# A recurrent attention stage on one Trainium2 core: which PSUM banks the gate exponents, the carried state's output and the output transposes share

## The chip, the core and the metric

One core of a Trainium2 chip runs the whole program. Five engines work in order, each through its own queue: TensorE (PE in the profile, with its weight loads as PEld), VectorE (DVE), ScalarE (ACT), GpSimd (POOL) and SyncE (SP, which only issues DMAs here; ACT's queue and POOL's issue some too). The metric is the device time of one execution in microseconds.

## The reference, cut to what matters

The first of three parts is a gated linear recurrence with a stabiliser; the other two (a routed expert layer and a two-branch product layer) run behind it and are not touched.

```python
m_new = np.maximum(f_gate[:, :, t] + m, i_gate[:, :, t])
f_stab = np.exp(f_gate[:, :, t] + m - m_new)
i_stab = np.exp(i_gate[:, :, t] - m_new)
C = f_stab[:, :, None, None] * C + i_stab[:, :, None, None] * np.einsum('bhd,bhe->bhde', vt, kt)
n = f_stab[:, :, None] * n + i_stab[:, :, None] * kt
h_tilde = np.einsum('bhde,bhe->bhd', C, qt)
denom = np.maximum(np.abs(nq), 1.0)          # nq = n . q
y[:, :, t] = o * h_tilde / denom             # o = sigmoid(o_gate)
```

There are 4 batches, 8 heads, 768 positions and 40 columns per head. The result, seen as 3072 tokens of 320 columns, goes into the router and the experts.

## The kernel before

The positions are cut into 6 chunks of 128. A step n (0 to 23) works on batch b = n mod 4 of chunk c = n // 4. Within a chunk the recurrence is a masked 128x128 product per head; the state carried from the chunk before adds its own part. One Python loop writes the order by hand: in step n the first two stages of step n+1 run beside the last stages of step n, the output of step n-2 is transposed and the router's logits of step n-3 are computed. No scheduler reorders anything, so every engine executes exactly what the loop wrote, and an instruction that waits stops all that is behind it on its engine.

The names that the text uses, with their lines:

- pe (L397) is the gate difference of four heads, one 512-column matmul; dd (L399, ACT) is its exponential, which POOL masks (L400). pq (L405) is q times k of the same heads, and P (L408, DVE) the product of pq and dd. Each step has two halves of all that (heads 0 to 3 and 4 to 7); they are called pe0, dd0, P0 and pe1, dd1, P1 here.
- pg (L421) is what the carried state gives, eight matmul records for four products; DVE scales it into num (L423).
- pv (L436) is P times v, pst (L442) the new state; DVE adds and copies them (L445, L453), and ACT spreads the state for the next chunk (Cb, L460).
- px (L485) are the output transposes of step n-2, copied by ACT to xt (L487, L488); pl (L495) are the logits of step n-3, copied by DVE into L (L496), the last DVE instruction that belongs to a step.
- pgt (L368, L369) are the gate transposes of the next chunk. They run in a gate step, the last of each chunk (n = 3, 7, 11, 15, 19); ACT copies them to gt (L371).
- Beside the steps the later layer's weights are converted from 64-bit words (`convs`, L119 to L153): DVE works on mu (L119, L122, L125), ACT rounds it (L131 or L152), POOL subtracts (L134, L136 or L153), and then DVE may start the next one. The gates of the next chunk (L293 to L358) run in the same gaps; ACT's hi (L316) and est (L353) belong to them.

PSUM has eight banks and all are taken: pst 1, pe 1, pq 2, pg 1, pv 1, and two for the tag `pxt`, which px, pl and pgt share. A tile that is allocated from a tag gets one of its buffers and has to wait until the last reader of the tile that was there has finished.

Of the kernel before, what the change touches and what calls it, by code (L numbers as in the profile page):

```python
# [6 lines left out]
F32 = mybir.dt.float32  # L7
# [14 lines left out]
T = 128  # L22
NC = S // T
DE = D + 1
# [19 lines left out]
class Kern:  # L44
# [173 lines left out]
    def attention(self, es):  # L218
# [6 lines left out]
        ps = es.enter_context(tc.tile_pool(name="aps", bufs=1, space=PSUM))  # L225
# [3 lines left out]
        def load_g(c):  # L229
            t = ld.tile([128, 2, T], F32, name="fi", bufs=2)  # L230
            nc.sync.dma_start(t, a["fi4"][:, c])
            FI[c] = t
# [28 lines left out]
        def load(n):  # L261
            c, b = divmod(n, B)
            t = qr[n % NQ]
            bd = t[:, H:].rearrange("p (a s) t -> p a s t", s=2)
            for s in range(2):
                r, rs = slice(64 * s, 64 * s + D), slice(D * s, D * s + D)
                nc.sync.dma_start(t[r, 0:H], a["qk"][rs, c, b])
                nc.sync.dma_start(bd[r, :, s], a["qk"][rs, c, b, 0:4])
            v_ = ld.tile([128, H, DE + D], F32, name="vk")
            nc.sync.dma_start(v_, a["vk"][b, c])  # L270
            VK[n] = v_

        def load_o(c):
            o_ = ld.tile([128, B, DM], F32, name="og", bufs=2)
            SG[c] = o_
            self.dma(lambda: nc.scalar.dma_start(o_, a["og"][:, c]))

        def sig(c):
            nc.scalar.activation(SG[c], SG[c], AF.Sigmoid)
            nc.scalar.activation(warm, gs[0:1, 0:1], AF.Exp)  # L280
# [83 lines left out]
        def gates2(c):  # L364
            est, mov, EW, md = GA[c]
            pg = ps.tile([128, 2 * T + 16], F32, tag="pxt", name="pgt", bufs=2)
            for i in range(2):
                nc.tensor.transpose(pg[:, i * T:(i + 1) * T], EW[:, i], identf)  # L368
            nc.tensor.matmul(pg[:, 2 * T:], psel, md, start=True, stop=True)  # L369
            gt = wk.tile([128, 2 * T + 16], F32, name="gt")  # L370
            nc.scalar.activation(gt, pg, AF.Copy)  # L371
            GA[c] = (est, mov, gt)

        def pre(n):
            c, b = divmod(n, B)
            est, mov, gt = GA[c]
            if c < NC - 1:
                wa = gt[:, T + 32 * b:T + 32 * b + 8]
                dec = gt[:, 2 * T + 4 * b:2 * T + 4 * b + 4]
                wv = wk.tile([128, H, DE], F32, name="wv")  # L380
                nc.gpsimd.tensor_tensor(wv, VK[n][:, :, 0:DE], wa[:, :, None].to_broadcast([128, H, DE]),
                                        op=OP.mult)
                ct = None
                if c:
                    ct = wk.tile([128, 4, DE], F32, name="ct")
                    nc.gpsimd.tensor_tensor(ct, Cc[:, b], dec[:, :, None].to_broadcast([128, 4, DE]), op=OP.mult)
                ST[n] = (wv, ct)

        def s1(n):
            c, b = divmod(n, B)  # L390
            est, mov = GA[c][0:2]
            qk = qr[n % NQ]
            P = wk.tile([128, H, T], F32, name="P", bufs=2)
            PT[n] = P
            for g in range(2):
                pe = ps.tile([128, 4, T], F32, name="pe", bufs=1)
                nc.tensor.matmul(pe, est[:, b], mov[:, 4 * g:4 * g + 4, :], start=True, stop=True)  # L397
                dd = wk.tile([128, 4, T], F32, name="dd", bufs=2)
                nc.scalar.activation(dd, pe, AF.Exp)  # L399
                nc.gpsimd.affine_select(dd, dd, pattern=[[0, 4], [1, T]], compare_op=OP.is_ge, fill=0.0,  # L400
                                        base=0, channel_multiplier=-1)
                pq = ps.tile([128, 4, T], F32, name="pq", bufs=2)
                for hp in (2 * g, 2 * g + 1):
                    o = 2 * (hp - 2 * g)
                    nc.tensor.matmul(pq[:, o:o + 2], qk[:, 4 + hp], qk[:, H + 2 * hp:H + 2 * hp + 2],  # L405
                                     start=True, stop=True)
                yield
                nc.vector.tensor_mul(P[:, 4 * g:4 * g + 4], pq, dd)  # L408
                yield
# [3 lines left out]
        def s2g(n):  # L413
            c, b = divmod(n, B)
            num = wk.tile([128, H, DE], F32, name="num", bufs=3)
            ND[n] = num
            if c:
                ea = GA[c][2][:, 32 * b:32 * b + 8]
                pg = ps.tile([128, 4, 2, DE], F32, name="pg")
                for hp in range(4):  # L420
                    nc.tensor.matmul(pg[:, hp], qr[n % NQ][:, hp], Cb[:, b, hp], start=True, stop=True)  # L421
                yield
                nc.vector.tensor_tensor(num, pg.rearrange("p a b d -> p (a b) d"),  # L423
                                        ea[:, :, None].to_broadcast([128, H, DE]), op=OP.mult)
# [55 lines left out]
        def s3(n):  # L480
            xf = XF.pop(n)
            px = ps.tile([128, 3 * T], F32, tag="pxt", name="px", bufs=2)
            for j in range(3):
                w = min(128, DM - 128 * j)
                nc.tensor.transpose(px[0:w, j * T:(j + 1) * T], xf[:, 128 * j:128 * j + w], identf)  # L485
            xt = xtb[n % 2]
            nc.scalar.activation(xt[:, 0:2], px[:, 0:2 * T], AF.Copy)  # L487
            nc.scalar.activation(xt[0:64, 2], px[0:64, 2 * T:3 * T], AF.Copy)  # L488
            XT[n] = xt

        def s4(n):
            xt = XT.pop(n)
            pl = ps.tile([128, 96], F32, tag="pxt", name="pl", bufs=2)
            for j in range(3):
                nc.tensor.matmul(pl, xt[:, j], wg[:, j], start=(j == 0), stop=(j == 2))  # L495
            return lambda: nc.vector.tensor_scalar(self.L[:, n], pl[:, 0:E], 0.0, None, op0=OP.add)  # L496
# [5 lines left out]
        def fill(k):  # L502
            j = 0
            while k and j < len(bg):
                v = next(bg[j], None)
                if v is None:
                    bg.pop(j)
                elif v == "w":
                    j += 1
                else:  # L510
                    k, j = k - 1, 0
# [5 lines left out]
        NS = B * NC  # L517
# [17 lines left out]
        for n in range(NS):  # L535
            c, b = divmod(n, B)
            if n == 2:
                bg.append(m2)
            if True:
                if n + 2 < NS:  # L540
                    load(n + 2)
                if n == 1:
                    next(m2)
                if b == 3 and c + 1 < NC:
                    gates2(c + 1)
                    if c + 2 < NC:
                        bg.insert(0, gates(c + 2))
                        if c + 3 < NC:
                            load_g(c + 3)
                m = s1(n + 1) if n + 1 < NS else iter(())  # L550
                next(m, None)
                g = s2g(n)
                next(g, None)
                fill(2)
                next(m, None)
                next(m, None)
                if n == 0:
                    sig(0)
                if b == 3 and c + 1 < NC:
                    sig(c + 1)  # L560
                self.drain()
                self.flush(b < 3)
                next(g, None)
                next(m, None)
                if n + 1 < NS:
                    pre(n + 1)
                g = s2(n)
                next(g)
                if 0 <= n - 2:
                    s3(n - 2)  # L570
                next(g)
                lc = s4(n - 3) if n >= 3 else lambda: None
                fill(2)
                next(g)
                fill(1)
                next(g)
                fill(1)
                next(g, None)
                lc()
            if n:  # L580
                xout(n - 1)
                if n % B == 0 and n // B + 1 < NC:
                    load_o(n // B + 1)
            if n - 3 == 7 or n - 3 == 15:
                bg.insert(0, self.keys(*KT[(n - 3) // 8]))
            fill(1)
# [643 lines left out]
```

## Time and profile before

| what | us |
|---|---|
| median of 3 timed runs (lowest, highest) | 911.85 (911.6, 914.33) |
| the profiled execution itself | 908.33 |
| its span in the profile | 906.6 |
| PE, DVE, ACT, POOL busy in the span | 822.6, 538.4, 353.3, 415.9 |
| mean granted clock of TensorE | 0.955 of full speed |

The attention stage takes about the first 196 us; the experts follow and keep PE busy nearly throughout. The profiled execution is one run, and its span leaves out 1.73 us around it. A row of the timeline gives the start, the duration and, in brackets, how long the engine had been idle before it and which instruction ended that. In the windows each engine has its busy time and, in brackets, its instructions.

### The profile page before, as it was taken

How to read it: one execution, taken by the hardware profiler on the slowest of the kernel's cores; microseconds unless marked ns; L12 is line 12 of the kernel's file. 1: busy time of each engine (PE TensorE's matmuls, PEld its weight loads, DVE VectorE, ACT ScalarE, POOL GpSimd, SP SyncE). 2: the span in 40 equal slices, each digit the busy share in tenths (PEclk: the TensorE clock that was granted, in tenths of full speed). 3: DMA queues.
4: the chain of work that ended last, by engine and by line, in shares of the span. 5: the costliest groups of instructions: out<-in, count | busy, mean ns of one | idle time of the engine just before them, and what ended most of it. 6: DMA issues, size and time to landing. Idle time of an engine off the chain costs nothing.

```text
span 906.6 us, 15898 instructions
## 1 busy us (share of the span) xinstructions
PE 822.6 (91%) x5939; PEld 780.7 (86%) x5939; DVE 538.4 (59%) x1188; ACT 353.3 (39%) x720; POOL 415.9 (46%) x441
## 2 busy tenths in 40 slices
PE   4889889976888799989989999999999999999996
PEld 3778788875777799979879998999899999999996
DVE  7678898756866974776576687476764212311211
ACT  4778777610443332232233234224322532532321
POOL 5577787621513670464056338233723823532122
PEclk9999999995889989979989999999999999999999
DMA  6877777413122310220120122031111301200000
GB/s 169 245 230 213 234 214 228 136 59 104 52 67 81 89 59 9 76 75 22 54 80 18 37 78 59 1 97 48 30 53 45 105 24 44 76 1 23 1 1 22
DMA packets 51037, 73.84 MB, mean 81 GB/s; under 512 B 6160, under 2 KB 41360, under 8 KB 50960
## 3 DMA queue, kind: packets, MB, share of 16 engines
q1 hardware_dynamic: 41744, 45.30, 17.7%
q10 hardware_dynamic: 6912, 19.66, 6.6%
q0 software_dynamic: 2304, 7.87, 2.7%
q8 instruction: 47, 0.77, 0.4%
q14 instruction: 30, 0.25, 0.1%
HBM read 63.37 MB, written 7.86 MB: 79 GB/s over the span
## 4 chain that ended last, share of the span: by engine, by line
PE 66%; DVE 15%; ACT 7%; issue 4%; DMA 4%; POOL 2%; SPq 0%; ACTq 0%; DVEq 0%; POOLq 0%
PE ring L983 33%; PE acc L983 20%; DVE G L661 4%; PE pq L405 2%; PE rt L685 2%; PE pv L436 2%; DVE w1h L920 1%; DMA qr<-in_qk_dram 1%; PE pl L495 1%; DMA vk<-in_vk_dram 1%; DVE gf L1106 1%; PE pe L397 1%; PE pg L421 1%; DMA mraw<-in_wab_dram 1%; ACT yh L979 1%
## 5 line engine op out<-in xcount | busy, mean ns | idle before, releaser
L1111 POOL TENSOR_TENSOR ml<-gf,mh 128x384 fp32r<-128x384 f32 x95 | 106.5, 1121 | 267.3 <-ACT mh L1108 266.8
L983 PE MATMUL ring<-yh,wh 128*128 128x384 f32 x576 | 203.5, 353 | 6.6 <-ACT yh L979 4.6
L983 PE MATMUL ring<-yl,wh 128*128 128x384 f32 x576 | 137.5, 345 | 0.0
L983 PE MATMUL ring<-yh,wl 128*128 128x384 f32 x384 | 133.7, 348 | 0.0
L1106 DVE TENSOR_TENSOR gf<-ring,at 128x384 f32<-128x384 f32 x96 | 53.3, 555 | 129.1 <-PE ring L983 125.0
L983 PEld LDWEIGHTS ring<-yh,wh 128*128 128x128 f32 x576 | 112.6, 196 | 14.1 <-ACT yh L979 7.2
L1108 ACT ACTIVATE mh<-gf 128x384 fp32r<-128x384 f32 x96 | 50.4, 525 | 189.7 <-DVE gf L1106 189.7
L661 DVE TENSOR_TENSOR G<-thc,d 128x1024 bf16<-128x1024 int16 (+1 forms) x90 | 109.6, 1236 | 0.4
L983 PEld LDWEIGHTS ring<-yl,wh 128*128 128x128 f32 x576 | 106.2, 194 | 0.0
L983 PE MATMUL acc<-woh,ml 128*128 128x320 f32 x288 | 91.5, 318 | 0.0
L983 PE MATMUL acc<-woh,mh 128*128 128x320 f32 x288 | 90.6, 315 | 0.0
L983 PE MATMUL acc<-wol,mh 128*128 128x320 f32 x288 | 90.4, 314 | 0.0
L983 PE MATMUL acc<-mh,w 128*128 128x384 f32 x320 | 88.4, 339 | 0.0
L1049 DVE SCALAR_TENSOR_TENSOR ml<-ring,mh 128x384 fp32r<-128x384 f32 x64 | 35.5, 556 | 80.3 <-ACT mh L1047 77.7
L1047 ACT ACTIVATE mh<-ring 128x384 fp32r<-128x384 f32 x64 | 31.4, 491 | 132.8 <-PE ring L983 126.8
L1104 ACT ACTIVATE at<-ring 128x384 f32<-128x384 f32 x96 | 46.8, 487 | 78.6 <-PE ring L983 76.8
L983 PEld LDWEIGHTS ring<-yh,wl 128*128 128x128 f32 x384 | 75.1, 195 | 0.0
L919 POOL TENSOR_TENSOR w1l<-raw,w1h 128x512 fp32r<-128x512 f32 x30 | 44.0, 1472 | 51.2 <-ACT w1h L915 51.2
L983 PE MATMUL ring<-xh,w1h 128*128 128x384 f32 x192 | 65.6, 342 | 0.1
L983 PE MATMUL acc<-ml,w 128*128 128x384 f32 x192 | 64.8, 338 | 0.8 <-DVE ml L1049 0.8
L983 PEld LDWEIGHTS acc<-mh,w 128*128 128x128 f32 x320 | 58.5, 189 | 0.2 <-issue 0.2
L983 PEld LDWEIGHTS acc<-woh,mh 128*128 128x128 f32 x288 | 55.1, 191 | 2.6 <-issue 2.6
(213 smaller groups left out, 1726.7 us busy)
## 6 DMA issues: line engine op xcount, KB each, us to landing
raw<-in_moe_w_dram SPq DMA_DIRECT2D x32, 320.0 KB
raw<-in_moe_w_dram SPq DMA_DIRECT2D x32, 256.0 KB
vk<-in_vk_dram SPq DMA_DIRECT2D x24, 324.0 KB
qr<-in_qk_dram SPq DMA_DIRECT2D x48, 160.0 KB
mraw<-in_wab_dram ACTq DMA_DIRECT2D x12, 640.0 KB
raw<-in_moe_w_dram SPq DMA_DIRECT2D x64, 64.0 KB
og<-in_og_dram ACTq DMA_DIRECT2D x6, 640.0 KB
qr<-in_qk_dram SPq DMA_DIRECT2D x48, 80.0 KB
```

The costliest lines, as they stand in the source:

```text
L405: nc.tensor.matmul(pq[:, o:o + 2], qk[:, 4 + hp], qk[:, H + 2 * hp:H + 2 * hp + 2], start=True, stop=True)
L436: nc.tensor.matmul(pvf[:, 64 * h:64 * h + w], P[:, h], vkf[:, (DE + D) * h:(DE + D) * h + w], start=True, stop=True)
L661: self.nc.vector.tensor_tensor(G, self.thc[:, None, 0:nthr].to_broadcast(dims), d[:, i0:i0 + 8, None].to_broadcast(dims), op=op)
L685: nc.tensor.matmul(cnt[0:nthr], Gs[j][:, i], oh[:, 8 * j + i], start=(j + i == 0), stop=(j * 8 + i == NT - 1))
L919: e.tensor_sub(l, raw[:, 0:2], h[:, 0:2].bitcast(F32))
L983: self.nc.tensor.matmul(*a, **k)
L1047: A.activation(hh, p, AF.Relu)
L1049: V.scalar_tensor_tensor(hl, p, 0.0, hh.bitcast(F32), op0=OP.max, op1=OP.subtract)
L1104: A.activation(at, p[0], AF.Copy)
L1106: V.tensor_mul(gf, p[1], at)
L1108: A.activation(gh, gf, AF.Copy)
L1111: e.tensor_sub(gl, gf, gh.bitcast(F32))
```

## The change

```diff
             for g in range(2):
-                pe = ps.tile([128, 4, T], F32, name="pe", bufs=1)
+                pe = ps.tile([128, 4, T], F32, name="pe", bufs=2)
...
             if c:
                 ea = GA[c][2][:, 32 * b:32 * b + 8]
-                pg = ps.tile([128, 4, 2, DE], F32, name="pg")
+                pg = ps.tile([128, 4, 2, DE], F32, tag="pxt", name="pg", bufs=2)
...
+                m = s1(n + 1) if n + 1 < NS else iter(())
+                next(m, None)
                 if b == 3 and c + 1 < NC:
                     gates2(c + 1)
...
-                m = s1(n + 1) if n + 1 < NS else iter(())
-                next(m, None)
                 g = s2g(n)
```

pe gets a second bank. For that pg gives up its own and is allocated from `pxt`, so pgt, pg, px and pl now share two banks. And in a gate step the first pe and pq of the next step are written ahead of the gate transposes. No instruction is added or removed, and the loads keep their places.

On PE this is the end of step 6 and the start of gate step 7 before the change (`pgt_879` is the tile of the gate transposes, `pg_897` that of the carried part, `pl_854` that of the logits; what stands in brackets is what the instruction waits for, by the engine that is waited for):

```order
L495 MATMUL pl_854<-wg_124,xt1_136 128x96 [waits DVE_49]
L495 MATMUL pl_854<-wg_124,xt1_136 128x96 x2
L368 MATMUL pgt_879<-identf_100,EW_571 128x128 [waits PE_49,Activation_49]
L368 MATMUL pgt_879<-identf_100,EW_571 128x128
L369 MATMUL pgt_879<-md_656,gs_122 128x16
L397 MATMUL pe_888<-mov_652,est_655 128x512
L405 MATMUL pq_893<-qr2_128 128x256 [waits DMAHW4_49,DMAHW3_49,DMAHW6_49,DMAHW0_49,DVE_49]
L405 MATMUL pq_893<-qr2_128 128x256
L421 MATMUL pg_897<-Cb_132,qr1_127 128x82 [waits DVE_49]
L421 MATMUL pg_897<-Cb_132,qr1_127 128x82 x3
L397 MATMUL pe_906<-mov_652,est_655 128x512 [waits Activation_49]
```

The same place after the change:

```order
L495 MATMUL pl_854<-wg_124,xt1_136 128x96 [waits DVE_49]
L495 MATMUL pl_854<-wg_124,xt1_136 128x96 x2
L397 MATMUL pe_880<-mov_652,est_655 128x512 [waits Activation_49]
L405 MATMUL pq_885<-qr2_128 128x256 [waits DMAHW4_49,DMAHW7_49,DMAHW3_49,DMAHW0_49]
L405 MATMUL pq_885<-qr2_128 128x256
L368 MATMUL pgt_888<-identf_100,EW_571 128x128 [waits PE_49,Activation_49]
L368 MATMUL pgt_888<-identf_100,EW_571 128x128
L369 MATMUL pgt_888<-md_656,gs_122 128x16
L421 MATMUL pg_897<-Cb_132,qr1_127 128x82 [waits Activation_49]
L421 MATMUL pg_897<-Cb_132,qr1_127 128x82 x3
L397 MATMUL pe_906<-mov_652,est_655 128x512
```

pe and pq stand ahead of the transposes; pe1 has lost its wait for ACT, and pg now waits for ACT, namely for the copy gt of the transposes just ahead of it, whose bank it takes.

One step on, in step 8, PE has before the change (`pl_949` are the logits computed in step 7, `pg_992` the carried part of step 8):

```order
L495 MATMUL pl_949<-wg_124,xt0_135 128x96 [waits DVE_49]
L397 MATMUL pe_983<-mov_652,est_655 128x512 [waits Activation_49]
L405 MATMUL pq_988<-qr0_126 128x256 [waits DMAHW4_49,DMAHW1_49,DMAHW7_49,DMAHW0_49,DVE_49]
L421 MATMUL pg_992<-Cb_132,qr2_128 128x82 [waits DVE_49]
L397 MATMUL pe_998<-mov_652,est_655 128x512 [waits Activation_49]
L405 MATMUL pq_1003<-qr0_126 128x256 [waits DVE_49]
```

And after it:

```order
L495 MATMUL pl_949<-wg_124,xt0_135 128x96 [waits DVE_49]
L397 MATMUL pe_983<-mov_652,est_655 128x512
L405 MATMUL pq_988<-qr0_126 128x256 [waits DMAHW4_49,DMAHW7_49,DMAHW3_49,DMAHW2_49]
L421 MATMUL pg_992<-Cb_132,qr2_128 128x82 [waits DVE_49]
L397 MATMUL pe_998<-mov_652,est_655 128x512 [waits Activation_49]
L405 MATMUL pq_1003<-qr0_126 128x256 x2
```

pg's wait for DVE reads alike and means another instruction. Before, it is L423 of step 7, the reader of pg's own bank. After, the built program puts pl_949 and pg_992 both in bank 2, and the count that pg waits for is that of L496 of step 7, which reads pl_949. The same holds in the steps 4, 12, 16 and 20, each the first of a chunk. In the other steps from 5 on that are no gate steps pg takes the bank of the px of the step before and waits for its copies (L487, L488), px takes the bank of that step's pl and waits for L496, and pl takes that of pg and waits for L423.

On ACT, a gate step's piece of the difference (`gt` is the copy of the gate transposes, `xt_135` that of the output transposes):

```order
 L487 ACTIVATE xt_135<-px 128x256
 L488 ACTIVATE xt_135<-px 64x128
+L399 ACTIVATE dd<-pe 128x512
 L371 ACTIVATE gt<-pgt 128x272
-L399 ACTIVATE dd<-pe 128x512 x2
+L399 ACTIVATE dd<-pe 128x512
```

The first exponential of the next step has moved ahead of the gate copy. DVE, POOL and SP have the same instructions in the same order.

## Rows read from the trace of the kernel before

**Rows 1.** Page, its first line: the span
```profile
span 906.6 us, 15898 instructions
```

**Rows 2.** Windows: stretch, length, busy PE, PEld, DVE, ACT, POOL, clock, DMA, GB/s
```profile
69.20:99.80 30.60, 26.96 (x243) 24.71 (x241) 25.46 (x58) 24.16 (x55) 24.81 (x31) 1.00 0.75 232
```

**Rows 3.** Waits of PE, first 200 us: total, times, longest
```profile
PE pe L397 <- ACT dd L399: 11.0, 12, 2.1
...
PE pgt L368 <- ACT xt L488: 6.0, 4, 2.3
```

**Rows 4.** Timeline of PE, steps 7 and 8: start, duration, what, [idle before <-releaser]
```profile
70.39 1.02 PE L421 MATMUL pg<-Cb,qr 128*128 128x82 f32 x8
71.20 0.48 PE L397 MATMUL pe<-mov,est 128*128 128x512 f32 x1
...
76.80 1.02 PE L421 MATMUL pg<-Cb,qr 128*128 128x82 f32 x8
78.06 0.49 PE L397 MATMUL pe<-mov,est 128*128 128x512 f32 x1 [0.24 <-ACT dd L399]
```

**Rows 5.** Timeline of DVE, end of step 7 and step 8
```profile
78.53 0.11 DVE L496 TENSOR_SCALAR L<-pl 128x8 f32<-128x8 f32 x1
...
83.17 1.01 DVE L119 TENSOR_SCALAR mu<-mraw 128x640 int32<-128x640 int32 x1 [1.19 <-POOL mtl L136]
```

**Rows 6.** Timeline of ACT, gate copy of step 7, last exponential of steps 7, 8
```profile
69.40 0.40 ACT L371 ACTIVATE gt<-pgt 128x272 f32<-128x272 f32 x1 [0.66 <-PE pgt L369]
...
71.71 0.60 ACT L399 ACTIVATE dd<-pe 128x512 f32<-128x512 f32 x1 [1.39 <-PE pe L397]
...
78.59 0.60 ACT L399 ACTIVATE dd<-pe 128x512 f32<-128x512 f32 x1 [0.58 <-PE pe L397]
```

**Rows 7.** Timeline of PE, the gate differences of steps 4, 12 and 20
```profile
45.29 1.01 PE L421 MATMUL pg<-Cb,qr 128*128 128x82 f32 x8
...
108.09 1.02 PE L421 MATMUL pg<-Cb,qr 128*128 128x82 f32 x8
...
171.68 1.02 PE L421 MATMUL pg<-Cb,qr 128*128 128x82 f32 x8
...
172.69 0.50 PE L397 MATMUL pe<-mov,est 128*128 128x512 f32 x1
```

**Rows 8.** Timeline of DVE, its logits copy at the end of steps 3, 11, 19
```profile
46.40 0.11 DVE L496 TENSOR_SCALAR L<-pl 128x8 f32<-128x8 f32 x1
...
111.03 0.11 DVE L496 TENSOR_SCALAR L<-pl 128x8 f32<-128x8 f32 x1
...
173.51 0.12 DVE L496 TENSOR_SCALAR L<-pl 128x8 f32<-128x8 f32 x1
```

**Rows 9.** Timeline of ACT, steps 4 and 12
```profile
47.08 0.60 ACT L399 ACTIVATE dd<-pe 128x512 f32<-128x512 f32 x1 [0.59 <-PE pe L397]
...
109.42 0.60 ACT L399 ACTIVATE dd<-pe 128x512 f32<-128x512 f32 x1 [0.78 <-PE pe L397]
...
111.42 0.42 ACT L316 ACTIVATE hi<-zs 128x256 fp32r<-128x256 f32 x1 [0.58 <-DVE zs L311]
...
115.57 1.28 ACT L353 ACTIVATE est<-es,gs 128x128 fp32r<-128x128 f32 x4 [0.61 <-DVE es L333]
```

**Rows 10.** Timeline of PE, step 6 and the gate transposes of step 7
```profile
64.53 0.49 PE L485 MATMUL px<-identf,x 128*128 128x128 f32 x3
...
68.80 0.44 PE L368 MATMUL pgt<-identf,EW 128*128 128x128 f32 x2 [1.66 <-ACT xt L488]
```

**Rows 11.** Timeline of DVE, the logits copy at the end of step 5
```profile
65.56 0.11 DVE L496 TENSOR_SCALAR L<-pl 128x8 f32<-128x8 f32 x1
```

**Rows 12.** Windows: a stretch behind a long wait of PE
```profile
118.00:124.00 6.00, 6.00 (x45) 5.57 (x46) 5.08 (x10) 5.22 (x15) 3.81 (x6) 0.72 0.89 296
```

**Rows 13.** Timeline of PE, that wait, and a slow gate difference later
```profile
117.96 0.51 PE L397 MATMUL pe<-mov,est 128*128 128x512 f32 x1 [2.07 <-ACT dd L399]
...
163.94 1.84 PE L421 MATMUL pg<-Cb,qr 128*128 128x82 f32 x8
```

## The prediction

> **What bounds the kernel now.** I read the page's first line for the span [rows 1], then the busy time by chunk, then what PE waits for, and then the timelines of PE, DVE and ACT side by side. The profiled execution took 908.33 us for a span of 906.6, so 1.73 lie around it. The change touches only the attention stage. There a chunk of four steps takes 30.60 us, in which PE is busy 26.96, DVE 25.46, POOL 24.81 and ACT 24.16 [rows 2]: no engine is full, and each is near enough to full that the chain runs through all of them. PE's waits are of two kinds: pe1 waits for the exponential that reads the only pe bank, 11.0 us in 12 places, and the gate transposes wait for the copies of px, 6.0 us in 4 places [rows 3]. Those are the waits that the change is about.
>
> The next thing to see is how far DVE is behind PE. In step 8 PE starts pg at 76.80 [rows 4], but DVE is still in step 7: L496, the last instruction of that step, reads the logits at 78.53 [rows 5]. The logits had been written in step 7. So DVE is 1.7 us behind at a point where PE owes it nothing. Today this lag costs nothing, as pg has a bank of its own.
>
> **The second pe bank** removes the 12 waits of pe1. Between them lie est, mov and the conversion on ACT, and ACT runs these in the same order as before; where pe1 waited longest (2.07 us, [rows 13]) it waited because ACT came late to dd0. PE gets there earlier and finds dd0 no earlier. Where ACT is idle between dd0 and dd1 only because pe1 had to run in between (0.58 us at 78.59 [rows 6], 0.59 at 47.08 and 0.78 at 109.42 [rows 9]) the second bank could save that idle time, unless pg, which stands ahead of pe1, holds it up. Bounds: from -11.0 us, if every wait of pe1 were the end of the chain, to 0. I take 0, since the places where ACT could start sooner are, but for such as lie ahead of a DMA that waits for POOL's x anyway, the ones where pg gets a new wait.
>
> **The new wait of pg in the first step of a chunk** (steps 4, 8, 12, 16, 20). pg takes the bank of the logits of the step before and waits for L496. Behind it on PE stand pe1, pq1 and pv; ACT waits for pe1 with dd1, and behind dd1 on ACT stand Cb, hi of the next gates and the conversion's rounding, for which POOL waits, for which DVE waits with L119.
>
> Step 8: L496 ends at 78.53 + 0.11 = 78.64; with the 0.05 that such a hand-over takes here (dd0 ended at 78.59 - 0.58 = 78.01, and pe1, which waited for it, started at 78.06 [rows 4, 6]), pg starts at 78.69 instead of 76.80. Undelayed, pe1 follows pg by 71.20 - 70.39 = 0.81 [rows 4], and dd1 follows pe1 by 71.71 - 71.20 = 0.51 [rows 4, 6]. So dd1 starts at 80.01 instead of 78.59: 1.42 us later. The way from there runs through ACT without idle time to the rounding, POOL, and L119 at 83.17, before which DVE waited 1.19 us for POOL alone [rows 5]. So all of the 1.4 arrives, and the rounds of the conversion carry it to the next chunk: what sets a round is DVE, ACT, POOL and DVE again, with no PE in it.
>
> Step 16 repeats step 8 with the same lag; I take 1.4.
>
> Step 4: L496 ends at 46.51 [rows 8], pg starts at 46.56 instead of 45.29 [rows 7], dd1 at 46.56 + 0.81 + 0.51 = 47.88 instead of 47.08 [rows 9]: 0.8. ACT later issues a DMA here that may take this up, so 0 to 0.8; I take 0.8.
>
> Step 12: DVE has the routing keys to do as well and is further behind. L496 ends at 111.14 [rows 8], pg starts at 111.19 instead of 108.09 [rows 7], dd1 at 112.51 instead of 109.42 [rows 9]: 3.1 on ACT. But ACT waits there anyway: 0.58 for hi and 0.61 for est, both for DVE [rows 9]. That leaves 3.1 - 1.19 = 1.9. DVE itself loses little; bounds 0.3 to 3.1, and I take 1.9, as est is on the way to dd0 of the step after.
>
> Step 20: L496 ends at 173.63 [rows 8], pg starts at 173.68 instead of 171.68 [rows 7], pe1 at 174.49 instead of 172.69: 1.8. Here the conversions end and PE alone sets the pace to the end of the stage, so all of it counts.
>
> Sum: 1.4 + 1.4 + 0.8 + 1.9 + 1.8 = 7.3 us.
>
> **The new waits elsewhere.** In the other steps px waits for L496 of the step before, and pl for L423 of its own. In step 6 px stands at 64.53 [rows 10] and L496 ends at 65.67 [rows 11], so PE stops for 1.2 us. In steps 5 to 7 and their likes PE has the room of the pe1 wait that is gone, and nobody waits for px or pst within 1.2 us, since DVE is behind: 0, and 1.2 at most where I am wrong.
>
> **The gate step.** pe0 and pq0 move ahead of the transposes, into the time in which these wait for the copies of px (1.66 us at 68.80 [rows 10]). From the transposes' start to pg lie 70.39 - 68.80 = 1.59, of which the transposes take 0.44 and pe0 and pq0 1.15. Up to 1.15 would be saved four times (step 3 has no such wait), -4.6. But PE comes to the place 1.2 later, for the px wait above: it was free at 68.80 - 1.66 = 67.14 and is now at 68.3; with pe0 and pq0, 69.5. The transposes start then, not at 68.80, and pg, in the transposes' own bank, waits for gt, which ends 69.80 - 68.80 = 1.00 behind their start [rows 6, 10]: 70.5, against 70.39 today. I take 0, with -4.6 and +0.4 (0.1 four times) as ends. What moves issues no DMA, so no queue of SP's or POOL's is passed; the loads of q that wait for a late pg are wanted a step later.
>
> So 7.3 us on the profiled execution's 908.33 is 915.6; on the median of the timed runs, 3.5 above it, 911.85 + 7.3 = 919.2.
>
> **The rivals.** *Faster: PE's own waits were the end of the chain.* Then the 11.0 us go: 900.9. For it speaks that the wait for dd is the largest one of PE [rows 3] and PE the busiest engine [rows 2]. This is also what the Trainium skill has (Perfetto Trace Analysis, "Matmuls"): independent matmul groups should rotate through different banks, so that one's evacuation lies beside the next one's matmuls. By that rule, taken for pe alone, the time would be 900.9; but the same rule speaks against pg, which goes from a bank of its own to one whose reader is late, and the rows of steps 7 and 8 agree with the second. It decides if DVE's L496 is done when PE comes to pg, that is, if DVE runs at least 1.9 us earlier in steps 8 and 16.
>
> *No change: the lag is taken up.* DVE, ACT and POOL have each some 5 us idle in a chunk [rows 2]. If DVE does its round sooner once it is let wait, for POOL beside it is then quieter, each delay shrinks to what a hand-over costs and the sum is within 2.7 us of 911.85. Against it: DVE's idle time sits ahead of L119, where it waits for POOL, which is behind the delay and not ahead of it.
>
> *Slower still: PE loses its clock in the new waits.* Behind its wait of 2.07 us at 117.96 [rows 13] the granted clock was 0.72 over the next six us [rows 12], part of them at the lower level of 1.2 GHz; behind that of 1.66 us at 68.80 it stayed at 1.00 [rows 2, 10]. The new waits are 1.9, 1.9, 2.0 and 3.1 us long. At the lower level pg took 1.84 instead of 1.02 us [rows 7, 13], so 0.82 more in steps 8, 12 and 16, and in step 20, where PE sets the pace, 6.0 x (1 - 0.72) = 1.7. That makes 4.2 more: 923.4. The Trainium skill describes such a kernel (TensorE: Matmul & The Clock Gate, "A second HAM failure mode: psum-queue depth-cycling"): PE idles a little between groups as it cycles through banks, and its clock goes to and fro. By it the sum would be this rival's; the rows of before show both outcomes at waits of about this length.
>
> **How the numbers follow.** The forecast has 0.60, slower with a cold clock 0.15, no change 0.13, faster 0.12. A difference of 0.3%, some 2.7 us, is about what a measurement of this kernel can tell from none. Hence slower 0.75, same 0.13, faster 0.12. The forecast's own ends: less 0.8 (step 4 taken up), 1.6 (step 12 at 0.3) and half of the gate steps' 4.6 it is 914.5, and with the clock 923.4. The range reaches from 911 to 924, which leaves out the faster rival and a small rest of the others.
>
> **What would show it.** In the profile after: PE's pg L421 waiting for DVE L496 in five places, for 1.3, 1.9, 3.1, 1.9 and 2.0 us; pe's waits for dd all but gone; ACT's dd1 in steps 8 and 16 waiting 2 us or more for PE; the last px of the stage some 7 us later and everything behind it moved by the same. The prediction is wrong if pg doesn't wait in steps 8 and 16, if L119 behind it comes no later than today, or if the stage ends earlier.

## The result, and the profile after

| | before | after |
|---|---|---|
| median of 20 runs each (lowest, highest), us | 909.62 (905.01, 914.51) | 917.94 (911.75, 922.68) |
| ratio, 95% interval | 1 | 1.0079 (1.0057 to 1.0101) |
| the profiled execution, us | 908.33 | 921.87 |
| its span, us | 906.6 | 920.2 |
| PE, DVE, ACT, POOL busy, us | 822.6, 538.4, 353.3, 415.9 | 830.6, 539.0, 353.8, 415.8 |
| mean granted clock of TensorE | 0.955 | 0.945 |

The changed kernel is slower by 8.3 us between the medians; the forecast was 7.3 slower. The two profiled executions lie 13.6 us apart, as that of after is one of the slower of its 20. So the profiles tell where the time goes, and the ratios how much it is.

The waits of PE after the change, first 210 us (what waited, for what, total us, times, longest), answer to [rows 3]:

```profile
PE px L485 <- DVE L L496: 7.0, 5, 1.6
PE pg L421 <- DVE L L496: 4.6, 4, 2.3
PE pl L495 <- DVE num L423: 4.4, 4, 1.9
...
PE pg L421 <- ACT gt L371: 1.9, 4, 0.5
...
PE pgt L368 <- ACT xt L488: 1.2, 2, 0.7
```

pe's 11.0 us for dd are gone without a rest, and those of the gate transposes for px's copies fell from 6.0 to 1.2. In their place stand 16.0 us for DVE (7.0 + 4.6 + 4.4), on three tiles: the three that go through the two shared banks in every step.

The timeline of PE after (start, duration, what, idle time before and what ended it), steps 4 to 20, answers to [rows 4, 7, 10]:

```profile
47.62 2.00 PE L421 MATMUL pg<-Cb,qr 128*128 128x82 f32 x8 [2.30 <-DVE L L496]
49.35 0.77 PE L397 MATMUL pe<-mov,est 128*128 128x512 f32 x1
...
68.72 0.52 PE L485 MATMUL px<-identf,x 128*128 128x128 f32 x3 [1.61 <-DVE L L496]
...
73.20 0.44 PE L368 MATMUL pgt<-identf,EW 128*128 128x128 f32 x2 [0.73 <-ACT xt L488]
74.26 1.12 PE L421 MATMUL pg<-Cb,qr 128*128 128x82 f32 x8 [0.49 <-ACT gt L371]
...
83.36 1.12 PE L421 MATMUL pg<-Cb,qr 128*128 128x82 f32 x8 [1.65 <-DVE L L496]
84.27 0.48 PE L397 MATMUL pe<-mov,est 128*128 128x512 f32 x1
...
114.97 0.97 PE L495 MATMUL pl<-wg,xt 128*128 128x96 f32 x6 [1.55 <-DVE num L423]
...
118.44 1.43 PE L421 MATMUL pg<-Cb,qr 128*128 128x82 f32 x8 [0.31 <-DVE L L496]
...
151.14 1.12 PE L421 MATMUL pg<-Cb,qr 128*128 128x82 f32 x8 [0.36 <-DVE L L496]
...
181.51 0.91 PE L495 MATMUL pl<-wg,xt 128*128 128x96 f32 x6 [1.93 <-DVE num L423]
...
183.65 1.12 PE L421 MATMUL pg<-Cb,qr 128*128 128x82 f32 x8
```

pg of the steps 4, 8, 12 and 20 starts 2.3, 6.6, 10.4 and 12.0 us later than in [rows 4, 7]. The stage ends 11.85 us later, which is most of the 13.6 us between the two profiled executions. Its last logits copy, before and then after:

```profile
196.70 0.17 DVE L496 TENSOR_SCALAR L<-pl 128x8 f32<-128x8 f32 x1 [1.60 <-PE pl L495]
```

```profile
208.55 0.17 DVE L496 TENSOR_SCALAR L<-pl 128x8 f32<-128x8 f32 x1 [1.60 <-PE pl L495]
```

What the late pg does to ACT and DVE is seen in step 8. ACT after, its second exponentials of steps 4, 8 and 12 (answers to [rows 6, 9]):

```profile
50.16 0.60 ACT L399 ACTIVATE dd<-pe 128x512 f32<-128x512 f32 x1 [2.75 <-PE pe L397]
...
84.79 0.60 ACT L399 ACTIVATE dd<-pe 128x512 f32<-128x512 f32 x1 [2.81 <-PE pe L397]
...
120.17 0.60 ACT L399 ACTIVATE dd<-pe 128x512 f32<-128x512 f32 x1 [3.12 <-PE pe L397]
```

And DVE after, its logits copy at the end of step 3, then the end of step 7 and step 8 (answers to [rows 5, 8]):

```profile
47.46 0.11 DVE L496 TENSOR_SCALAR L<-pl 128x8 f32<-128x8 f32 x1
...
83.20 0.11 DVE L496 TENSOR_SCALAR L<-pl 128x8 f32<-128x8 f32 x1
...
86.23 0.69 DVE L408 TENSOR_TENSOR P<-pq,dd 128x512 f32<-128x512 f32 x1 [1.14 <-PE pq L405]
...
89.33 0.50 DVE L445 TENSOR_TENSOR num<-num,pv 128x328 f32<-128x328 f32 x1 [1.75 <-PE pv L436]
89.75 0.64 DVE L119 TENSOR_SCALAR mu<-mraw 128x640 int32<-128x640 int32 x1
```

This is the loop of the loss. PE waits for DVE's L496 until 83.36; ACT then waits 2.81 us for PE, and DVE itself 1.14 and 1.75 us for PE, where before it had its work ready and waited for POOL alone. Each engine waits for the next once around. L119 comes at 89.75 instead of 83.17, 6.6 us later; 4.7 of these L496 has already, and step 8 adds 1.9. Not all of it need be the bare wait: the granted clock was 0.81 from 80 to 88 us and 0.67 from 44 to 54 us (rows at e4), and pg of step 4 took 2.00 us instead of 1.01.

### The profile page after: what moved, and what is told of

Its sections match the earlier page's. It is cut to its first block, busy times and chain, and to the rows that moved or that the text cites. A ratio compares the mean times of both kernels' runs of the same rounds, so it can differ in the third digit from the quotient of the medians.

```text
span 920.2 us, 15924 instructions
## 1 busy us (share of the span) xinstructions
PE 830.6 (90%) x5939; PEld 784.4 (85%) x5939; DVE 539.0 (59%) x1188; ACT 353.8 (38%) x720; POOL 415.8 (45%) x441
## 4 chain that ended last, share of the span: by engine, by line
PE 62%; DVE 20%; issue 7%; POOL 5%; ACT 4%; DMA 1%; ACTq 0%; DVEq 0%; POOLq 0%; SPq 0%
PE ring L983 32%; PE acc L983 19%; DVE G L661 4%; PE rt L685 2%; PE pv L436 2%; PE pq L405 2%; DVE w1h L920 1%; POOL dd L400 1%; PE pg L421 1%; DVE gf L1106 1%; DVE mu L122 1%; PE pl L495 1%; DVE mu L119 1%; POOL x L475 1%; ACT yh L979 1%
## 5 line engine op out<-in xcount | busy, mean ns | idle before, releaser
L1047 ACT ACTIVATE mh<-ring 128x384 fp32r<-128x384 f32 x64 | 31.5, 492 | 134.8 <-PE ring L983 130.2
L405 PE MATMUL pq<-qr 128*128 128x256 f32 x192 | 55.9, 419 | 3.3 <-DMA qr<-in_qk_dram 3.3
```

Of the source, the lines that this page charges most:

```text
L1047: A.activation(hh, p, AF.Relu)
```

## The experiments

Ratios are to runs of the kernel before that were taken beside each group of experiments; their median was 910.48 us for e1 to e4, 911.72 for e5 to e8, 911.25 for e9 to e11. The theory at the start: pg stands behind a bank that DVE reads late. The rivals: the clock that falls in the new waits, the move, the second pe bank, and sharing as such.

**e1: the move alone.**

```diff
+                m = s1(n + 1) if n + 1 < NS else iter(())
+                next(m, None)
                 if b == 3 and c + 1 < NC:
                     gates2(c + 1)
...
-                m = s1(n + 1) if n + 1 < NS else iter(())
-                next(m, None)
                 g = s2g(n)
```

> The kernel before with only the written order changed: in a gate step pe0 and pq0 of the next step stand ahead of the gate transposes; pg keeps its own bank, pe has one. Theory (pg waits for the late logits copy): the cost is not here, the ratio to before lies between 0.995 and 1.001 (up to 4 times 1.15 us saved). Rival (the move delays the gate copy gt, and with it the gates): most of the 8 us are here, ratio 1.005 or more.

Measured: 907.94 us, ratio 0.9963 (0.994 to 0.9986): a gain of some 3.4 us. PE in its gate step 7:

```profile
67.78 0.44 PE L368 MATMUL pgt<-identf,EW 128*128 128x128 f32 x2 [0.52 <-ACT xt L488]
68.19 1.10 PE L421 MATMUL pg<-Cb,qr 128*128 128x82 f32 x8
```

The transposes' wait is 0.52 instead of 1.66 us [rows 10], and pg comes at 68.19 instead of 70.39 [rows 4]; 0.9 of these 2.2 us this execution has already at pg of step 4 (44.41 instead of 45.29). By itself the move is no part of the loss.

**e2: both pools, the order of before.**

```diff
-                pe = ps.tile([128, 4, T], F32, name="pe", bufs=1)
+                pe = ps.tile([128, 4, T], F32, name="pe", bufs=2)
...
-                pg = ps.tile([128, 4, 2, DE], F32, name="pg")
+                pg = ps.tile([128, 4, 2, DE], F32, tag="pxt", name="pg", bufs=2)
```

> The changed kernel with the written order of before: two pe banks and pg in the shared banks, the gate transposes first in a gate step. Theory: pg still waits for the logits copy of the step before in steps 4, 8, 12, 16 and 20, so the ratio to before stays at 1.006 to 1.010, pg's waits for L496 sum to 4 us or more. Rival (the move): ratio within 1.000 +- 0.002.

Measured: 919.55 us, 1.0089 (1.0059 to 1.0119). Without the move the loss is the same within the interval: where pg shares, the move's gain is not seen. The loss is in the two pools.

**e3: the change, with the logits read early.** It leaves the banks as they are and takes away DVE's lag at this one reader.

```diff
                 next(g)
+                lc()
                 fill(1)
...
                 next(g, None)
-                lc()
```

> The changed kernel, and DVE copies the logits (L496) right behind its addition L445, ahead of the denominator and of the gates and conversion work that the loop puts between; every bank is then free earlier. Theory: pg's and px's waits for L496 (4.6 and 7.0 us in the trace) fall under 2 us together and the loss goes: ratio 0.994 to 1.002. Rival (PE's clock or the move): the ratio stays at 1.005 to 1.010, as neither is touched.

Measured: 909.23 us, 0.9988 (0.9969 to 1.0006). PE's waits, first 210 us:

```profile
PE pg L421 <- DVE L L496: 9.0, 8, 1.7
PE pl L495 <- DVE num L423: 5.1, 7, 1.5
```

The loss went, the wait did not: pg waits for L496 in 8 places and for 9.0 us. I had expected under 2. With the copy at another place of the order the tiles fall on the banks otherwise, and pg follows a pl more often; but px no longer waits for L496, and the longest of pg's waits is 1.7 instead of 2.3. So a total of PE's waits is not the price. e6 and e7 show how much of this gain the copy has by itself.

**e4: work in the wait.** pq0 is computed three times in the steps 4, 8, 12, 16 and 20, ahead of pg's wait (that of the next step, whose number n is here; lines move by one: L421 is L422, L496 is L497).

```diff
-                for hp in (2 * g, 2 * g + 1):
+                rep = 3 if g == 0 and n > 4 and n % B == 1 else 1
+                for hp in (2 * g, 2 * g + 1) * rep:
```

> The changed kernel, and in steps 4, 8, 12, 16 and 20 PE repeats pq0 twice more (four matmuls, some 1.7 us, the same result again) ahead of pg, so that PE works instead of idling while it waits for the logits copy. Rival (the clock falls in those waits and costs 4 us): pg of step 4 takes 1.0 instead of 2.0 us and the ratio to before falls from 1.008 to 1.003 to 1.006. Theory (the wait itself costs, the clock little): the ratio stays within 0.002 of 1.008, or rises by up to 0.002 where the work is longer than the wait.

Measured: 918.35 us, 1.0084 (1.0052 to 1.0115). The windows (stretch, length, busy PE, PEld, DVE, ACT, POOL, granted clock, DMA, GB/s), first of the changed kernel:

```profile
44.00:54.00 10.00, 7.70 (x32) 6.71 (x32) 7.38 (x20) 5.90 (x17) 3.69 (x5) 0.67 0.53 142
...
80.00:88.00 8.00, 6.35 (x35) 5.50 (x34) 5.98 (x19) 5.10 (x16) 2.52 (x5) 0.81 0.49 161
```

then with the wait filled:

```profile
44.00:54.00 10.00, 9.03 (x75) 8.07 (x74) 7.79 (x22) 6.26 (x17) 4.45 (x7) 1.00 0.62 162
78.00:88.00 10.00, 10.00 (x81) 9.23 (x81) 7.32 (x21) 7.67 (x23) 5.09 (x7) 1.00 0.60 185
```

and its pg of step 4:

```profile
48.68 1.12 PE L422 MATMUL pg<-Cb,qr 128*128 128x82 f32 x8 [0.97 <-DVE L L497]
49.59 0.48 PE L397 MATMUL pe<-mov,est 128*128 128x512 f32 x1
```

Of the logits copies on DVE, those of steps 3, 7, 11 and 19, and of PE's pg, that of steps 12 and 20:

```profile
48.51 0.11 DVE L497 TENSOR_SCALAR L<-pl 128x8 f32<-128x8 f32 x1
...
80.66 0.11 DVE L497 TENSOR_SCALAR L<-pl 128x8 f32<-128x8 f32 x1
...
113.37 0.10 DVE L497 TENSOR_SCALAR L<-pl 128x8 f32<-128x8 f32 x1
...
177.86 0.12 DVE L497 TENSOR_SCALAR L<-pl 128x8 f32<-128x8 f32 x1
```

```profile
114.52 1.02 PE L422 MATMUL pg<-Cb,qr 128*128 128x82 f32 x8
...
179.81 1.01 PE L422 MATMUL pg<-Cb,qr 128*128 128x82 f32 x8
```

The clock stays at 1.00 (2.4 GHz) where it had fallen to 0.67, pg takes 1.12 instead of 2.00 us, and the time is the same, as the theory had it. That doesn't show that the fallen clock is free. The repeats are longer than the wait: in steps 12 and 20 pg starts 1.05 and 1.83 us after the copy has ended, so this run takes the cold clock away and adds work of its own. And in the profiles the chunk from the copy of step 3 to that of step 7 is 32.13 us long before (46.40 to 78.53 [rows 5, 8]), 35.74 in the changed kernel (47.46 to 83.20) and 32.15 here (48.51 to 80.66), though pg of step 4 waits for the copy here too. So in these two executions the loss of this chunk is gone together with the cold clock. But this execution is one of the faster of its kernel (915.37 against a median of 918.35) and that of the changed kernel one of the slower. How much of the loss is the bare wait and how much the clock that falls in it stays open.

**e5: pg shares, but among three banks** (one pe bank, order of before).

```diff
-                pg = ps.tile([128, 4, 2, DE], F32, name="pg")
+                pg = ps.tile([128, 4, 2, DE], F32, tag="pxt", name="pg", bufs=3)
...
-            px = ps.tile([128, 3 * T], F32, tag="pxt", name="px", bufs=2)
+            px = ps.tile([128, 3 * T], F32, tag="pxt", name="px", bufs=3)
```

(pgt and pl likewise.)

> The kernel before, in its own order and with one pe bank; pg's own bank is put into the shared pool, which so has three banks for pgt, pg, px and pl. Three tiles go through it in a step, so that pg comes back to the bank of the pg of the step before and waits for its reader, L423, as with a bank of its own. Theory (what costs is the bank of a tile that DVE reads late, not that tiles share): ratio 0.998 to 1.002, PE's waits for L496 in front of pg none, pe's waits for dd still about 11 us. Rival (any turn-taking of pg with px and pl couples the steps): 1.004 or more.

Measured: 907.3 us, 0.9943 (0.9914 to 0.9972), outside both expectations, on the faster side. PE's waits, first 215 us:

```profile
PE pe L397 <- ACT dd L399: 9.4, 10, 2.1
...
PE pg L421 <- ACT xt L488: 1.6, 3, 0.8
```

Sharing as such doesn't cost. What it gains fits the gate transposes: with three banks they need not follow a px that is still being read. PE of this kernel at the end of step 6:

```profile
65.19 0.91 PE L495 MATMUL pl<-wg,xt 128*128 128x96 f32 x6
65.94 0.38 PE L368 MATMUL pgt<-identf,EW 128*128 128x128 f32 x2
```

They start at 65.94 right behind the logits and not at 68.80 [rows 10]: the same 6.0 us of [rows 3] that the move goes for.

**e6: the early copy alone; e7: with the move.** The edit of e3 on the kernel before, in e7 with that of e1.

> The kernel before with one edit: the copy of the logits (L496) is written right behind the sums L445 that stand ahead of it in the step, earlier in DVE's order. It shows whether the early copy is a gain by itself, or only takes the wait away that the change made. Theory (it heals the wait): 0.998 to 1.002. Rival (DVE's order at the end of a step is itself the bound, and the early copy would have sped up any kernel): 0.994 or less.

> The kernel before with pe and pq of a gate step moved ahead of the gate transposes, and the early copy of the logits; pg has a bank of its own and pe has one bank. Beside the run with the whole change and the early copy (0.9988) it gives what the second pe bank is worth when the shared bank no longer hurts. Theory (the second pe bank is worth nothing): the same as the move alone, 0.994 to 0.998. Rival (the second bank is worth some of its 11 us, hidden by what is left of the waits): 1.000 or more here.

Measured: 909.44 us, 0.9954 (0.9926 to 0.9982), and 905.37 us, 0.9937 (0.9906 to 0.9968), at the lower edge of what I expected. The early copy is a gain by itself, between my theory and its rival. By medians it is only 909.44 / 911.72 = 0.9975, and its profiled execution, with a span of 907.9, doesn't show where it would be; how much it is, and by what, stays open. So of the 0.9% that it saved in e3 (1.0079 to 0.9988) up to half need not be the healing of a wait. And e3 is e7 with the second pe bank and the shared pg: 0.9988 against 0.9937, 0.5% slower. Reading the logits early takes about half of the harm and not all: beside the move alone (0.9963) the changed kernel is 1.2% slower.

**e8: the logits have a bank to themselves,** pgt, pg and px take turns in the other.

```diff
-            pl = ps.tile([128, 96], F32, tag="pxt", name="pl", bufs=2)
+            pl = ps.tile([128, 96], F32, name="pl", bufs=1)
...
-                pg = ps.tile([128, 4, 2, DE], F32, tag="pxt", name="pg", bufs=2)
+                pg = ps.tile([128, 4, 2, DE], F32, tag="pga", name="pg", bufs=1)
...
-            px = ps.tile([128, 3 * T], F32, tag="pxt", name="px", bufs=2)
+            px = ps.tile([128, 3 * T], F32, tag="pga", name="px", bufs=1)
```

(pgt as pg.)

> The whole change, but with the two shared banks divided otherwise: the logits pl have one to themselves, and pgt, pg and px take turns in the other. pg then waits for the copies of px on ACT (or for gt in a gate step), px for L423 of its own step, and pl for L496 of the step before; pe has its two banks. Theory (the loss is pg's place behind the late copy L496): most of it goes, 0.997 to 1.003, and pg no longer waits for L496. Rival (any sharing by pg costs, whoever reads the bank): 1.005 or more, with waits of pg for the copies of px, or of px for L423, of some 7 us in all.

Measured: 927.33 us, 1.0149 (1.0107 to 1.0191): against the theory. PE's waits, first 215 us:

```profile
PE px L485 <- DVE num L423: 19.8, 8, 3.6
...
PE pg L421 <- ACT xt L488: 2.1, 2, 1.5
```

pg no longer waits for L496, as expected; but px now comes to the bank that pg has just left and waits for L423 of its own step. DVE is late with that one too, and the wait is longer. The theory was too narrow: it is not L496, it is any reader that is late, and how soon PE comes back to the bank.

**e9: pg with the gate transposes, px with pl.** Here pg has nearly a bank of its own, and pe has two.

```diff
-                pg = ps.tile([128, 4, 2, DE], F32, tag="pxt", name="pg", bufs=2)
+                pg = ps.tile([128, 4, 2, DE], F32, tag="pga", name="pg", bufs=1)
...
-            px = ps.tile([128, 3 * T], F32, tag="pxt", name="px", bufs=2)
+            px = ps.tile([128, 3 * T], F32, tag="pxl", name="px", bufs=1)
...
-            pl = ps.tile([128, 96], F32, tag="pxt", name="pl", bufs=2)
+            pl = ps.tile([128, 96], F32, tag="pxl", name="pl", bufs=1)
```

(pgt as pg.)

> The whole change, with the two shared banks divided a third way: pg takes turns with the gate transposes pgt alone, px and pl with each other. pg then waits for its own reader L423 of the step before, as in the kernel before, and for gt in a gate step; px waits for L496 of the step before, pl for the copies of the px just ahead of it; pe has its two banks, the gate step its new order. Theory (the loss is pg and px tied to each other and to the late DVE; the second pe bank by itself neither costs nor gives): as the move alone, 0.993 to 0.999; waits of pl for the copies of px under 0.5 us each, of px for L496 some 2 us in all. Rival (a second pe bank lets PE run ahead into DVE's lag whatever shares, and so costs): 1.003 or more, with px waiting for L496 7 us or more in all. Second rival (the second pe bank is worth its waits once nothing ties pg): 0.990 or less.

Measured: 942.09 us, 1.0329 (1.0294 to 1.0365). It missed by far, and through a wait that I had put at 0.5 us. PE's waits, first 225 us:

```profile
PE pl L495 <- ACT xt L488: 31.5, 18, 2.8
```

pl follows px in one bank with only pv and pst between, and ACT's copies of px are not done when PE comes back: 31.5 / 18 = 1.75 us each time. Now it is a reader on ACT that is late. On the worth of a second pe bank this run says nothing.

**e10: pg in the two shared banks and nothing else** (one pe bank, order of before).

> The kernel before with pg in the two shared banks and nothing else: one pe bank, its own order. With the run of both pools without the move (1.0089) it tells what the second pe bank adds to the loss. Theory (the loss is the sharing alone): 1.006 to 1.011, pe's waits for dd still 8 us or more. Rival (the second pe bank is part of the loss, since PE comes earlier to pg): 1.004 or less.

Measured: 917.45 us, 1.0082 (1.0054 to 1.0111), as expected. PE's waits, first 215 us:

```profile
PE pe L397 <- ACT dd L399: 6.1, 10, 1.5
PE pg L421 <- DVE L L496: 5.8, 4, 2.7
...
PE px L485 <- DVE L L496: 4.6, 4, 1.2
PE pl L495 <- DVE num L423: 3.8, 2, 2.3
```

pe's waits were left in, 6.1 us (I had expected 8 or more). The shared bank alone is the whole loss; with the second pe bank it was 1.0089 (e2), so where pg shares that bank gives nothing that can be measured (the two intervals leave some 4 us either way).

**e11: three shared banks, the move and the early copy,** with one pe bank.

> A version from what the runs pointed to: one pe bank, pg in a shared pool of three banks (0.9943 alone), pe and pq of a gate step ahead of the gate transposes (0.9963 alone), the early copy of the logits (0.9954 alone). If the three act on different waits they add up to 0.986; theory: the first two take away the same wait of the gate transposes (6.0 us) and so count once, which leaves 0.990 to 0.995.

Measured: 906.99 us, 0.9939 (0.9905 to 0.9974). The gains don't add up, as expected if the move and the third bank take away the same wait. e7, e11 and e5 can't be told apart (905.37, 906.99, 907.3 us); each beats the kernel before by some 0.6% and the changed one by 1.4%. e7 is the simplest: pg and pe keep one bank each, pe and pq go ahead of the gate transposes, and the logits are read early.

## Why the prediction was right

*Which term carries the loss.* The sum had 7.3 us for pg's new place, 0 for the second pe bank, 0 for the move beside it. Taken apart: pg's place alone 1.0082, some 7.5 us (e10); with the second pe bank 1.0089 (e2); with the move 1.0079. All three terms hold within their intervals, which leave some 3 to 4 us for each of the two zeros.

*The second pe bank at 0.* pe's waits went, 11.0 to none, and the time with them did not. In their place stands pg: in step 8 dd1 waits 2.81 us for pe1 because pg, which waits for L496, stands ahead of pe1. What a second pe bank gives where pg does not share, no run shows. The rotation of banks that the Trainium skill asks for (Perfetto Trace Analysis, "Matmuls") gave here just what the trace bore out: nothing for pe, whose reader sits in a chain that ran on without PE's wait, and a loss for pg, whose new bank has a late reader.

*The new wait of pg.* The place and the reader were right, the sizes per step were not. Forecast were waits of 1.3, 1.9, 3.1, 1.9 and 2.0 us, 10.2 in all; the trace has 2.30, 1.65, 0.31, 0.36 and none listed, 4.6. Where pg waited less, PE had been stopped ahead of it: by pl for L423 (1.55 us in front of step 12, 1.93 in front of step 20) and by px for L496. Step 16 was to repeat step 8; there pg waited 0.36 us and dd1 0.76 instead of 2 or more. What I had followed was one tile against a DVE that I left where it was before; but PE is held by the same DVE at all three tiles, and whichever comes first takes the wait.

*The new waits elsewhere at 0.* This is the step that was wrong in kind: "nobody waits for px or pst within 1.2 us". px waits 7.0 and pl 4.4 us, and DVE waits for pv and pq behind them. They stand where pg's waits fell short, so that the sum came out near is in part luck. No run takes the waits of px, pl and pg apart; in e3 pg waited 9.0 us, twice as long, and the loss was gone. Nor does the loss grow as forecast: pg comes 2.3 us late in step 4, 6.6 in step 8, 10.4 in step 12, 12.2 in step 16 (151.14 against 138.94) and no later in step 20, which was to add 1.8. Of the 2.3 in step 4, 1.06 are not the change's wait: L496 of step 3 is late by as much (47.46 against 46.40), in the first chunk, in which no pg runs. e5, which loses nothing, has this copy at 47.64.

*The move at 0.* The ends were -4.6 and +0.4. Alone it gives -3.4 (e1). In the changed kernel it gives nothing that can be measured (1.0079 against 1.0089), by the way that the prediction had: px is held 1.61 us in front of it (68.72), and pg waits 0.49 for gt behind it (74.26).

*The rivals.* That PE's own waits were the end of the chain falls with e2. That the lag is taken up falls with the result: DVE, once it lets PE wait, waits itself for PE (1.14 and 1.75 us in step 8) and gets no earlier. The cold clock did come, 0.67 in the ten microseconds around step 4. That it came on top of the forecast's 7.3 us and made 4.2 more is not what the medians have; how much of the 8.3 us is its part stays open (e4). The Trainium skill's case of a clock that goes to and fro as PE cycles through PSUM banks (TensorE: Matmul & The Clock Gate, "A second HAM failure mode: psum-queue depth-cycling") agrees with the clock seen here; whether with a cost too, e4 leaves open.

## What to carry to other kernels

Before tiles are put into a common pool, write down for each the reader that frees its bank, how late that reader's engine runs at the place where the next tile takes it, and how much work of the writing engine lies between. With three tiles of a step in three banks sharing cost nothing here (0.9943), in two 0.8%, with px one tile behind pg in one bank 1.5%, with pl right behind px 3.3%. A wait that is large in the profile is worth a bank only if what stands behind it isn't late for another reason: pe's 11.0 us were worth nothing that could be measured where pg shared, the gate transposes' 6.0 us some 3.4 (e1).

## What the runs showed that was not expected

- PE's clock can stay low for longer than the wait ahead of it: in e8, behind 2.42 us in front of px, PE ran at 0.57 of full speed over eight microseconds, most of them at the 1.2 GHz level. The window, and three instructions of it:

```profile
92.00:100.00 8.00, 7.50 (x47) 6.91 (x48) 5.96 (x12) 4.31 (x11) 6.25 (x7) 0.57 0.68 240
```

```profile
92.50 0.87 PE L485 MATMUL px<-identf,x 128*128 128x128 f32 x3 [2.42 <-DVE num L423]
95.61 1.60 PE L495 MATMUL pl<-wg,xt 128*128 128x96 f32 x6
96.91 0.77 PE L397 MATMUL pe<-mov,est 128*128 128x512 f32 x1
```

  pl took 1.60 and pe 0.77 us there, against 0.91 and 0.47 at full clock. What of the 1.5% this is was not tried.
- With work put into the waits the clock was 1.00 in both stretches shown and the median the same; in its profile the chunk behind the first wait was as long as before (e4).
- Executions of one kernel on one core spread by 9.5 us (before) and 10.9 us (after) over 20 runs, so that two single profiles, 13.6 us apart, told 5 us more than the medians.
